# Row softmax steps on GpSimd and convolution evacuations on ScalarE, in a convolution and soft-MoE kernel

## The chip, the cores and the metric

One core of one Trainium2 chip runs the whole program. The metric is the device time of one execution in microseconds. TensorE (PE) multiplies matrices from SBUF into PSUM; VectorE (DVE) and ScalarE (ACT) copy PSUM to SBUF ("evacuate") and do elementwise work; GpSimd (POOL) works on SBUF; SyncE (SP) issues the DMAs.

## The reference

The input x is 8 batches of 3584 rows of 192 columns. A causal convolution over 7 rows, with one softmaxed set of weights for each of 8 heads (24 columns each), gives the rows of a soft mixture of experts with 32 slots (8 experts of 4 slots, hidden size 1024). The weights of the convolution are drawn eight times larger than in the function below.

```python
def _moe_ref(x, phi, w1, w2):
    logits = x @ phi                              # 28672 x 32
    d = softmax of logits over the 28672 rows     # dispatch
    slot_input = d.T @ x                          # 32 x 192
    slot_out[e] = relu(slot_input[e] @ w1[e]) @ w2[e]
    c = logits - logits.max(1, keepdims=True)     # row softmax over 32 slots
    c = np.exp(c)
    c /= c.sum(1, keepdims=True) + 1e-09
    return c @ slot_out                           # 28672 x 192
```

The row softmax c, in the last lines, is what the change touches first: one softmax over 32 numbers for each of the 28672 rows.

## The kernel before

All data are float32. The work of a batch is cut in two halves (n = 0 to 15 for 8 batches).

- **Convolution.** The even half of a batch uses `conv` (one 128x128 Toeplitz matrix a head, L522), the odd half `conv_units` (64x64 matrices, two heads at a time, L491, "units"). Results go through four PSUM banks `cv0` to `cv3` and are evacuated into the tiles `xc`. `conv` evacuates on ACT alone; `conv_units` on ACT or DVE. The copies are recorded at the helper's lines: L248 for ACT, L250 for DVE.
- **Turn and logits.** DVE transposes `xc` in 32x32 blocks into `xt` (L574, L580), PE computes the logits of the batch into the four banks of `lt` (L605).
- **Dispatch (`stage_b`).** DVE reads the logits, writes their negatives to `lall` and takes a running extremum (L629, L633); ACT takes the exponential into `dt` (L639); PE transposes it (L677); two copies of 128x512 bring it to SBUF as `dsb`, on ACT or DVE; PE accumulates the slots with it (L700) and DVE adds them to `ss` (L717).
- **Row softmax (`epath(j, u)`).** For each half batch u of batch j, 16 "softmax halves" in all, on 128x448 elements of `lall` in place: transpose (DVE, L763), minimum (L765), subtraction (L769), exponential (ACT, L773), sum, plus 1e-9 and reciprocal (DVE, L756 to L758), multiplication (L777), transpose back (L780). The small results lie in the tile `rmr`. This needs the logits of its batch and is needed only by the output of its batch.
- **Experts.** After the last batch the slots are normalized, multiplied with w1 and w2 (L871, L875, L916), scaled into `os` (L929) and spread over the partitions as `st` (L934).
- **Output.** For each batch PE multiplies `lall` with `st` (L957), alternating between the `cv` and the `lt` banks; ACT or DVE evacuates into `xc` buffers, which hold two batches; SP stores them (L982), 22 MB in all.

A planner fixes the order of instructions on every engine. Each step is added with a cost for each engine that may do it, the steps that it depends on, and a priority; where two engines may do a step, the planner takes the one that ends earlier by its costs. Steps with a priority of 1500 or more (the row softmax and the output) are fitted afterwards into the gaps that the others leave; POOL's memsets (x halo L460, L861) are planned in the same way. At run time every engine follows its order strictly, with semaphores between engines.

Of the kernel before, what the change touches and what calls it, by code (L numbers as in the profile page):

```python
# [12 lines left out]
ALU = mybir.AluOpType  # L13
# [4 lines left out]
class Plan:  # L18
# [16 lines left out]
    def add(self, fn, cost, reads=(), writes=(), prio=0.0, bias=0.15):  # L35
        i = len(self.steps)
        deps = set()
        for r in reads:
            if r in self.writer:
                deps.add(self.writer[r])  # L40
        for w in writes:
            if w in self.writer:
                deps.add(self.writer[w])
            deps.update(self.readers.get(w, ()))
        for r in reads:
            self.readers.setdefault(r, []).append(i)
        for w in writes:
            self.writer[w] = i
            self.readers[w] = []
        deps.discard(i)  # L50
        self.steps.append((fn, cost, deps, prio, bias, self.urgent))
        return i
# [125 lines left out]
def tile_conv_softmoe(ctx: ExitStack, tc: tile.TileContext, x, weight, phi, w1, w2, out):  # L178
    nc = tc.nc
# [34 lines left out]
    GT = TG * M  # L214
    NR = GT // RUN
    assert S == NG * GT and NR == P and HALO >= ZS
    NP = NT // 2
# [7 lines left out]
    def a_ps(n):  # L225
        return (n + 61) / 1200

    def a_sb(n):
        return (n + 112) / 1200

    def v_ps(n):
        return (n + 64) / 960

    def v_sb(n):
        return (n + 66) / 960
# [4 lines left out]
    def evac(n):  # L240
        return {"ACT": a_ps(n), "DVE": v_ps(n)}
# [4 lines left out]
    def copy(e, dst, src):  # L246
        if e == "ACT":
            nc.scalar.copy(dst, src)  # L248
        else:
            nc.vector.tensor_copy(dst, src)  # L250
# [17 lines left out]
    ltk, nvk = [f"lt{i}" for i in range(NB)], [f"ltn{i}" for i in range(NB)]  # L268
# [121 lines left out]
    for i in range(len(cuts) - 1):  # L390
# [3 lines left out]
            writes=[f"prod{i}"] + (alll + ["scr"] if i == 0 else []), prio=-3 + i,  # L394
        )
        add(band_sum(i), {"DVE": v_sb(HH * BW * KT)}, reads=[f"prod{i}"], writes=[f"band{i}"], prio=-3 + i)
        for u in range(2):
            for a, b in tk[u]:
                add(
                    band_put(i, a, b, u), {"ACT": a_sb(HH * U * 0.7), "DVE": v_sb(HH * U * 0.7)},  # L400
                    reads=[f"band{i}", ("tz", "tzu")[u], "scr"] + alll,
                    writes=[f"toe{'pu'[u]}{h}.{a}{b}" for h in range(cuts[i], cuts[i + 1])], prio=-3 + i + 6 * u,
# [65 lines left out]
    def rot(name, n):  # L468
        k = ring.get(name, 0)
        ring[name] = k + 1  # L470
        return f"{name}{k % n}"
# [7 lines left out]
    def conv_units(ch):  # L479
        pr = ch["n"] * 5  # L480
        CW = 2 * CG
        for h in range(0, H, 2):
            banks = [rot("cv", 4) for _ in range(2)]
            d0, d1 = h * CG, h * CG + CW
            pv = [ps[b][:, 0 : NP * CW].rearrange("p (q c) -> p q c", c=CW) for b in banks]

            def mm(e, h=h, pv=pv):
                for hh in range(h, h + 2):
                    for s, a in ((0, 0), (1, 1), (0, 1), (1, 0)):
                        rows = slice(UW * s, UW * (s + 1))  # L490
                        nc.tensor.matmul(  # L491
                            pv[s][UW * a : UW * (a + 1), :, (hh - h) * CG : (hh - h + 1) * CG], toeu[rows, hh, :],
                            ch["x"][rows, a:NT:2, hh * CG : (hh + 1) * CG], start=True, stop=True,
                        )

            add(
                mm, {"PE": 2 * NP * CG / 600 + 0.05},
                reads=[ch["xk"], ch["xk"] + "z"] + [f"toeu{hh}.{a}{b}" for hh in (h, h + 1) for a, b in tk[1]],
                writes=banks + [f"hd{ch['n']}.{hh}" for hh in (h, h + 1)], prio=pr,
            )  # L500
            for s in range(2):
                for w, lo, hi, o in (("a", d0, min(d1, P), s * (W2 - P)), ("b", max(d0, P), d1, 1 + s * D2)):
                    if lo >= hi:
                        continue

                    def ev(e, s=s, lo=lo, hi=hi, o=o, pv=pv, d0=d0):
                        copy(e, ch["xc"][:, :, o + lo : o + hi], pv[s][:, :, lo - d0 : hi - d0])

                    add(
                        ev, evac(NP * (hi - lo)), reads=[banks[s], "one"], writes=[f"{ch['xck']}.{h}{w}{s}"],  # L510
                        prio=pr,
                    )

# [72 lines left out]
    def stage_b(hs_):  # L586
# [3 lines left out]
        n, last = hs_[-1]["n"], hs_[-1]["n"] == 2 * B - 1  # L590
        tb, si, W = j * GT, len(stages), 4 * (h1 - h0) * U
        pr = n * 5 + 4.5
# [6 lines left out]
        for k in range(DB):  # L599

            def lg(e, k=k):
# [13 lines left out]
                reads=["phi"] + pace + [f"xt{hf}.{s}" for hf in range(h0, h1) for s in ((0, 1) if 32 * k < P else (2, 3))]  # L615
# [4 lines left out]
        lo = lall[:, tb : tb + GT].rearrange("p (r n b) -> p b n r", r=RUN, b=NB)[:, :, 4 * i0 : 4 * i1, :]  # L620
# [16 lines left out]
        for a0, a1 in parts:  # L637
# [6 lines left out]
                writes=[f"dt.{i}" for i in range(a0, a1, 4)], prio=pr,  # L644
# [28 lines left out]
        for a0, a1 in parts:  # L673

            def dtr(e, a0=a0, a1=a1):
# [5 lines left out]
                writes=nvk[a0 // 2 : a1 // 2], prio=late,  # L681
            )
        for b in range(i0 // 2, i1 // 2, 2):
            add(
                lambda e, b=b: copy(
                    e, dsb.rearrange("p (b k) n -> p b (k n)", k=2)[:, b : b + 2, :], nv[:, b : b + 2, :]
                ),
                evac(512), reads=nvk[b : b + 2], writes=[f"ds{b}"], prio=pr,
            )


        for a0, a1 in parts:

            def disp(e, a0=a0, a1=a1):
# [13 lines left out]
                reads=[f"ds{b}" for b in range(a0 // 2, a1 // 2, 2)] + ka, writes=[ltk[0], nvk[0]], prio=late,  # L708
# [36 lines left out]
    def epath(j, u, p0):  # L745


        n = 2 * j + u
        pr, GT = p0 + 20 * j, NR * RUN // 2
        lv = lall[:, n * GT : (n + 1) * GT]  # L750
        ev = lv.rearrange("p (a n) -> p a n", n=NS)
        rv, rk, lk = rmr[:, n % 4, 0 : GT // NS], f"r{n % 4}", f"l{j}.{u}"
        rb = rv.unsqueeze(2).broadcast_to((P, GT // NS, NS))

        def total(e):
            nc.vector.tensor_reduce(out=rv, in_=ev, axis=AX.X, op=ALU.add)  # L756
            nc.vector.tensor_scalar(out=rv, in0=rv, scalar1=1e-9, scalar2=None, op0=ALU.add)  # L757
            nc.vector.reciprocal(rv, rv)  # L758


        lp = lv.rearrange("p (t m b) -> p t b m", m=4, b=NB)
        ln = lv.rearrange("p (t b m) -> p t b m", m=4, b=NB)
        add(lambda e: nc.vector.transpose(ln, lp), {"DVE": v_sb(GT)}, reads=[lk], writes=[lk], prio=pr)  # L763
        add(
            lambda e: nc.vector.tensor_reduce(out=rv, in_=ev, axis=AX.X, op=ALU.min),  # L765
            {"DVE": v_sb(GT) + 0.1}, reads=[lk], writes=[rk], prio=pr,
        )
        add(
            lambda e: nc.vector.tensor_tensor(out=ev, in0=ev, in1=rb, op=ALU.subtract),  # L769
            {"DVE": v_sb(GT)}, reads=[lk, rk], writes=[lk], prio=pr,  # L770
        )
        add(
            lambda e: nc.scalar.activation(lv, lv, AF.Exp, scale=-1.0), {"ACT": a_sb(GT)}, reads=[lk], writes=[lk], prio=pr  # L773
        )
        add(total, {"DVE": v_sb(GT) + 0.4}, reads=[lk], writes=[rk], prio=pr)
        add(
            lambda e: nc.vector.tensor_tensor(out=ev, in0=ev, in1=rb, op=ALU.mult),  # L777
            {"DVE": v_sb(GT)}, reads=[lk, rk], writes=[lk], prio=pr,
        )
        add(lambda e: nc.vector.transpose(lv, lv), {"DVE": v_sb(GT)}, reads=[lk], writes=[lk], prio=pr)  # L780

# [6 lines left out]
    for n in range(2 * B + 1):  # L788
        if n == 2 * B - 1:
            plan.urgent = 0.4  # L790
        if n < 2 * B:
            (conv, conv_units)[n % 2](halves[n])
            if n + 3 < 2 * B:
                load_x(halves[n + 3])
        if n:
            ch = halves[n - 1]
            turn(ch)
            if ch["hf"]:
                stage_b(halves[n - 2 : n])
# [12 lines left out]
    for j in range(B):  # L812
        for u in range(2):
            epath(j, u, 1975 - 10 * u)
# [70 lines left out]
    op = ps["lt0"]  # L885
    for hf in range(HF):
# [24 lines left out]
        def l2(e, hf=hf):  # L911
# [14 lines left out]
            writes=["lt0"], prio=301.5,  # L926
# [17 lines left out]
    for j in range(B):  # L944
        tb = j * GT
        pr = 2000 + 20 * j + 5
        obs = [flat(xcr[(2 * j + a) % 4])[:, 0 : 2 * RUN * D].rearrange("p (k i d) -> p k i d", i=RUN, d=D) for a in range(2)]
        for i0 in range(0, RUN, 2):
            i1 = min(RUN, i0 + 2)
            banks = pok[npo % 2]  # L950
# [13 lines left out]
            for g in range(NG):  # L964
# [6 lines left out]
                w = [f"ob{oc}.{k}.{i0}"]  # L971
# [4 lines left out]
                if i1 in cutsw:  # L976

                    def store(e, g=g, k=k, lo=cutsw[i1], hi=i1, ob=obs[g // 2], j=j):
# [5 lines left out]
                    lo = cutsw[i1]  # L984
                    add(
                        store, dma((i1 - lo) * P * D * 4, (i1 - lo) * D * 4),
                        reads=[f"ob{oc}.{k}.{i}" for i in range(lo, i1, 2)], prio=pr + 0.1 * g,
# [31 lines left out]
```

## Time and profile before

| | |
|---|---|
| median of 3 runs | 265.89 us (262.21 to 265.9) |
| the profiled execution's own time | 263.53 us |
| its span | 261.7 us, 8162 instructions |
| busy time in the span | PE 213.6, DVE 196.8, ACT 110.0, POOL 7.2 us |
| mean granted TensorE clock | 0.854 |
| moved by DMA | 60.32 MB, 22.02 MB of it written |

A row of a timeline gives start, duration, engine, line, operation, tiles (out<-in) and count, and in brackets how long the engine stood idle before it and what released it. A table by stretches gives for each the busy time of each engine, with the number of instructions, then the granted clock, the share of the DMA engines' time and the GB/s.

The stages are: set-up to 18 us, a first batch filling the pipeline to 35, the loop over batches to about 155, the last dispatch and the experts to 192, the output to the end.

### The profile page before, as it was taken

What the parts mean: (1) busy time and instruction counts of PE and PEld (TensorE: products, weight loads), DVE (VectorE), ACT (ScalarE), POOL (GpSimd) and SP (SyncE); (2) the same over time, 40 slices, a digit from 0 to 9 for tenths busy, and PEclk for the clock granted to TensorE, in tenths of its full rate; (3) what the DMA queues carried; (4) which work ended last, traced back from release to release, by engine and by line L of the source; (5) the groups of instructions that cost most, each with busy time, mean ns of one, the idle gap of its engine ahead of it and who ended that gap; (6) DMA issues with size and microseconds to landing.
All of it is one profiled execution on the core that took longest, in us unless ns stands there. A gap on an engine that the chain in (4) does not pass through costs nothing. (4 is left out here: it accounts for less than half of the span.)

```text
span 261.7 us, 8162 instructions
## 1 busy us (share of the span) xinstructions
PE 213.6 (82%) x3474; PEld 129.5 (49%) x3474; DVE 196.8 (75%) x368; ACT 110.0 (42%) x277; POOL 7.2 (3%) x31
## 2 busy tenths in 40 slices
PE   6577999989989999999899787589777776786750
PEld 6334355355454464463463365455456655565630
DVE  3959299879889989989789579667878676974340
ACT  2675364363353454534445150422146443543340
POOL 5000000000000000000000002000000000000000
PEclk9689999999999999999999899689979755555555
DMA  5999969689489599499399879200028998797897
GB/s 165 248 262 237 274 161 238 206 185 281 181 194 285 206 217 336 138 222 295 82 231 247 269 241 347 87 3 3 3 90 285 360 395 334 286 372 297 337 350 271
DMA packets 52851, 60.32 MB, mean 230 GB/s; under 512 B 4304, under 2 KB 45136, under 8 KB 52816
## 3 DMA queue, kind: packets, MB, share of 16 engines
q1 hardware_dynamic: 52816, 59.81, 76.9%
q8 instruction: 27, 0.44, 0.7%
q14 instruction: 8, 0.07, 0.1%
HBM read 37.78 MB, written 22.02 MB: 228 GB/s over the span
## 5 line engine op out<-in xcount | busy, mean ns | idle before, releaser
L248 ACT COPY xc<-cv 128x384 f32<-128x384 f32 (+1 forms) x162 | 69.3, 456 | 85.9 <-PE cv L522 45.4
L522 PE MATMUL cv<-x,toep 128*128 128x384 f32 x128 | 57.3, 549 | 5.3 <-DMA x<-in_x_dram 3.5
L574 DVE STREAM_TRANSPOSE xt<-xc 128x1024 f32<-128x1024 f32 x32 | 37.9, 1221 | 9.5 <-PE lt L605 6.6
L957 PE MATMUL cv<-st,lall 32*128 32x192 f32 x256 | 33.0, 509 | 6.6 <-ACT xc L248 4.0
L605 PE MATMUL lt<-xt,phiq 32*32 32x224 f32 x1536 | 33.0, 360 | 5.0 <-issue 2.7
L522 PEld LDWEIGHTS cv<-x,toep 128*128 128x128 f32 x128 | 21.3, 197 | 27.7 <-issue 14.3
L957 PEld LDWEIGHTS cv<-st,lall 32*128 32x128 f32 x256 | 25.8, 286 | 11.6 <-ACT xc L248 7.0
L250 DVE COPY xc<-lt 128x192 f32<-128x192 f32 (+2 forms) x42 | 16.4, 422 | 18.9 <-ACT xc L248 16.0
L491 PE MATMUL cv<-x,toeu 64*64 64x192 f32 x512 | 29.9, 345 | 0.4 <-DVE xc L250 0.4
L250 DVE COPY xc<-cv 128x384 f32<-128x384 f32 (+2 forms) x54 | 25.0, 482 | 4.8 <-ACT xc L248 2.2
L957 PE MATMUL lt<-st,lall 32*128 32x192 f32 x192 | 21.5, 508 | 7.7 <-DVE xc L250 6.1
L605 PEld LDWEIGHTS lt<-xt,phiq 32*32 32x32 f32 x1536 | 12.9, 103 | 30.0 <-issue 22.6
L700 PE MATMUL lt<-xc,dsb 128*32 128x193 f32 x512 | 24.0, 342 | 3.5 <-DVE dsb L250 2.3
L491 PEld LDWEIGHTS cv<-x,toeu 64*64 64x64 f32 x512 | 19.9, 138 | 9.7 <-ACT xc L248 4.5
L700 PEld LDWEIGHTS lt<-xc,dsb 128*32 128x32 f32 x512 | 16.3, 114 | 12.6 <-DVE dsb L250 5.8
L957 PEld LDWEIGHTS lt<-st,lall 32*128 32x128 f32 x192 | 16.2, 294 | 11.7 <-ACT xc L248 5.7
L580 DVE STREAM_TRANSPOSE xt<-xc 128x512 f32<-128x512 f32 x32 | 20.6, 678 | 0.0
L248 ACT COPY xc<-lt 128x384 f32<-128x384 f32 (+2 forms) x30 | 10.8, 376 | 22.6 <-PE lt L957 15.6
L629 DVE TENSOR_SCALAR_CACHE_REDUCE lall<-lt 128x896 f32<-128x896 f32 x8 | 13.9, 1736 | 7.0 <-PE lt L605 7.0
L763 DVE STREAM_TRANSPOSE lall<-lall 128x448 f32<-128x448 f32 x16 | 15.2, 961 | 0.0
L639 ACT ACTIVATE dt<-lt,small 128x896 f32<-128x896 f32 (+1 forms) x9 | 8.2, 925 | 12.1 <-DVE lall L629 9.9
L677 PE MATMUL lt<-ident,dt 128*128 128x128 f32 x64 | 9.6, 298 | 3.9 <-ACT dt L639 3.9
(95 smaller groups left out, 166.2 us busy)
## 6 DMA issues: line engine op xcount, KB each, us to landing
x<-in_x_dram SPq DMA_DIRECT2D x64, 192.0 KB, 4.7
x<-in_x_dram SPq DMA_DIRECT2D x24, 384.0 KB, 6.5
out_dram<-xc SPq DMA_DIRECT2D x24, 384.0 KB, 4.1
out_dram<-xc SPq DMA_DIRECT2D x24, 288.0 KB, 3.8
x<-in_moe_w_dram SPq DMA_DIRECT2D x6, 768.0 KB, 6.7
out_dram<-xc SPq DMA_DIRECT2D x24, 192.0 KB, 2.0
w1a<-in_moe_w_dram SPq DMA_DIRECT2D x8, 512.0 KB, 8.0
x<-in_x_dram SPq DMA_DIRECT2D x8, 288.0 KB, 5.2
```

The source lines that it names most:

```text
L248: nc.scalar.copy(dst, src)
L250: nc.vector.tensor_copy(dst, src)
L491: nc.tensor.matmul(pv[s][UW * a : UW * (a + 1), :, (hh - h) * CG : (hh - h + 1) * CG], toeu[rows, hh, :], ch["x"][rows, a:NT:2, hh * CG : ...
L522: nc.tensor.matmul(pv, toep[:, h, :], ch["x"][:, :, d0:d1], start=True, stop=True)
L574: lambda e, s=s, o=o: nc.vector.transpose(xa[:, s, :, :, 0:P], xg[:, :, :, o : o + P]),
L580: lambda e, s=s, o=o: nc.vector.transpose(xa[:, s, :, :, P:D], xg[:, :, :, o : o + D2]),
L605: nc.tensor.matmul(lt[g * NS : (g + 1) * NS, b, 0:W], phiq[rows, k, :], xt[rows, h0:h1, 4 * g : 4 * g + 4, 32 * k : 32 * k + U], start=(k ...
L629: nc.vector.tensor_scalar(out=lo, in0=li, scalar1=-1.0, scalar2=None, op0=ALU.mult, op1=ALU.min, accum_out=cm)
L677: nc.tensor.transpose(nv[:, i // 2, i % 2 * P : (i % 2 + 1) * P], dt_[:, i, :], ident)
L700: nc.tensor.matmul(sp[g * NS : (g + 1) * NS, o : o + D1], dsb[:, i, g * NS : (g + 1) * NS], xc[:, 2 * g + k, s * D1 : (s + 1) * D1], start ...
L763: add(lambda e: nc.vector.transpose(ln, lp), {"DVE": v_sb(GT)}, reads=[lk], writes=[lk], prio=pr)
L957: nc.tensor.matmul(ps[banks[g]][:, (i - i0) * 256 : (i - i0) * 256 + D], lall[rows, tb + i * NR : tb + (i + 1) * NR], st[rows, :], start=T ...
```

## The change

Three edits. The evacuations of `conv_units` may be done on ACT only. The copies into `dsb` may be done on ACT only, except for the last batch's. The subtraction (L769) and the multiplication (L777) of the row softmax go from DVE to POOL, with a planned cost of 1.0 us each; before, the planned cost on DVE was (448 + 66)/960, 0.54 us. The planner makes a new order with these costs.

```diff
 # conv_units
                     add(
-                        ev, evac(NP * (hi - lo)), reads=[banks[s], "one"], writes=[f"{ch['xck']}.{h}{w}{s}"],
+                        ev, {"ACT": a_ps(NP * (hi - lo))}, reads=[banks[s], "one"], writes=[f"{ch['xck']}.{h}{w}{s}"],
                         prio=pr,
                     )
 # stage_b
-                evac(512), reads=nvk[b : b + 2], writes=[f"ds{b}"], prio=pr,
+                evac(512) if last else {"ACT": a_ps(512)}, reads=nvk[b : b + 2], writes=[f"ds{b}"], prio=pr,
 # epath
         add(
-            lambda e: nc.vector.tensor_tensor(out=ev, in0=ev, in1=rb, op=ALU.subtract),
-            {"DVE": v_sb(GT)}, reads=[lk, rk], writes=[lk], prio=pr,
+            lambda e: nc.gpsimd.tensor_tensor(out=ev, in0=ev, in1=rb, op=ALU.subtract),
+            {"POOL": 1.0}, reads=[lk, rk], writes=[lk], prio=pr,
         )
...
         add(
-            lambda e: nc.vector.tensor_tensor(out=ev, in0=ev, in1=rb, op=ALU.mult),
-            {"DVE": v_sb(GT)}, reads=[lk, rk], writes=[lk], prio=pr,
+            lambda e: nc.gpsimd.tensor_tensor(out=ev, in0=ev, in1=rb, op=ALU.mult),
+            {"POOL": 1.0}, reads=[lk, rk], writes=[lk], prio=pr,
         )
```

## The prediction

> **What bounds the kernel now.** I read the page's span first, then the stages: a table of busy times by stretch (columns: stretch, its length, then PE, PEld, DVE, ACT, POOL busy with instruction counts, granted clock, DMA share, GB/s).
>
> ```profile
> span 261.7 us, 8162 instructions
> ...
> 35.00:155.00 120.00, 112.02 (x2136) 58.66 (x2132) 103.04 (x164) 55.02 (x125) 1.24 (x5) 0.99 0.85 225
> 155.00:192.00 37.00, 28.38 (x582) 18.61 (x586) 30.03 (x66) 7.85 (x21) 1.81 (x1) 0.91 0.26 87
> 192.00:207.00 15.00, 12.32 (x150) 10.39 (x150) 10.83 (x24) 8.17 (x21) 0.00 (x0) 0.77 0.71 258
> 207.00:216.00 9.00, 6.54 (x56) 4.95 (x56) 7.14 (x13) 4.38 (x12) 0.00 (x0) 0.64 1.02 394
> 216.00:237.00 21.00, 15.92 (x130) 12.13 (x130) 16.19 (x37) 9.25 (x24) 0.00 (x0) 0.50 0.84 324
> 237.00:252.00 15.00, 11.34 (x111) 9.88 (x112) 6.96 (x16) 6.33 (x16) 0.00 (x0) 0.50 0.89 342
> ```
>
> The loop over the batches (35 to 155 us) is PE's: 112.0 of 120 us at full clock, so at most 8 us can be won there, whatever happens to DVE, which is 86% busy, or ACT, at 46%. From 192 us on the output is written. At 207 to 216 us the DMA engines are full (394 GB/s); after that they have holes (0.84, 0.89), PE runs at half clock, and the two stretches differ in one thing: up to 237 us DVE still does softmax work between the evacuations. How much, the instructions that touch the small statistics tile rmr show (six of the eight DVE steps of one softmax half, so 96 for 16 halves):
>
> ```profile
> 35.00:155.00 120.00, 19.32 (x40) 0.99 0.85 225
> 155.00:192.00 37.00, 14.71 (x33) 0.91 0.26 87
> 192.00:262.00 70.00, 11.36 (x24) 0.58 0.84 316
> ```
>
> 24 of 96, so four halves' worth of sixteen, are done while output is being written. What they cost there is read from PE, in order of time: each of these rows is the start of a batch of output, with the wait in front of it (the first three at higher clock, before DMA limits; the batch between 202.27 and 220.38 has no such clean row).
>
> ```profile
> 191.86 1.20 PE L957 MATMUL cv<-st,lall 32*128 32x192 f32 x16 [0.41 <-ACT st L248]
> ...
> 197.03 1.41 PE L957 MATMUL cv<-st,lall 32*128 32x192 f32 x16
> ...
> 202.27 1.82 PE L957 MATMUL cv<-st,lall 32*128 32x192 f32 x15
> ...
> 220.38 1.66 PE L957 MATMUL lt<-st,lall 32*128 32x192 f32 x16 [1.43 <-ACT xc L248]
> ...
> 229.30 1.66 PE L957 MATMUL lt<-st,lall 32*128 32x192 f32 x16 [1.41 <-DVE xc L250]
> ...
> 238.15 1.66 PE L957 MATMUL lt<-st,lall 32*128 32x192 f32 x16 [1.45 <-DVE xc L250]
> ...
> 246.13 1.66 PE L957 MATMUL lt<-st,lall 32*128 32x192 f32 x16 [1.42 <-DVE xc L250]
> ```
>
> A batch takes 8.92 and 8.85 us while softmax halves are in the way, 7.98 us when they are done, at the same clock of 0.50. 22.02 MB in 8 batches at 394 GB/s is 6.99 us of DMA each, so PE and its evacuations set the pace after 216 us.
>
> **The change, part by part.** First POOL's price. The trace of before has no two-input POOL instruction; the rows nearest to it, and the DVE rows it replaces (columns: line, engine, operation, shapes, count | busy us, mean ns | idle before):
>
> ```profile
> L769 DVE TENSOR_TENSOR lall<-lall,rmr 128x448 f32<-128x448 f32 x16 | 9.9, 616 | 0.2
> ...
> L777 DVE TENSOR_TENSOR lall<-lall,rmr 128x448 f32<-128x448 f32 x16 | 10.0, 624 | 0.4
> ...
> L861 POOL MEMSET xc<- 128x2048 f32 x1 | 1.8, 1810 | 44.8 <-PE lt L700 44.8
> ...
> L321 POOL MEMSET toep<- 128x1024 f32 x1 | 0.9, 945 | 0.0
> ...
> masks.py:199 POOL TENSOR_SCALAR_AFFINE_SELECT ident<-ident 128x128 f32<-128x128 f32 x1 | 0.3, 292 | 0.1
> ```
>
> The memsets give 0.845 ns an element ((1810-945)/1024) and 80 ns fixed, so 448 elements cost at least 0.46 us. The select, which reads and writes, takes (292-80)/128 = 1.66 ns an element; two reads at twice that give 3.3 ns, 1.56 us, the upper end. I take the select plus one more stream at the memsets' rate, 2.5 ns: 1.2 us. It hides nowhere by itself, since it stands in a chain (minimum, subtract, exponential, sum, scale, transpose), but the halves have until 192 us and other work lies on every engine meanwhile; 32 x 1.2 = 38 us on an engine that is now 3% busy.
> The Trainium skill, GPSIMD Engine Reference, section 3.1, measures 4497 ns for such an instruction of 2048 elements, as an estimate 984 ns for 448; its section 4.1 says not to put elementwise work there, being about twice as slow as VectorE. No run here shows it yet; by its figure the sum stays the same, since both prices lie below the point at which the slower rival starts.
>
> DVE's budget in the loop. Moved away are its 33 PSUM copies there and 40/96 of L769 and L777 (19.9 us), 8.3 us. These copies, and the transposes that stay:
>
> ```profile
> 35.00:155.00 120.00, 14.63 (x33) 0.99 0.85 225
> ...
> L763 DVE STREAM_TRANSPOSE lall<-lall 128x448 f32<-128x448 f32 x16 | 15.2, 961 | 0.0
> ...
> L780 DVE STREAM_TRANSPOSE lall<-lall 128x448 f32<-128x448 f32 x16 | 10.3, 643 | 0.4
> ```
>
> 14.6 + 8.3 = 22.9 us come free, beside 17 us that are idle now. A half costs DVE 45.38/16 = 2.84 us of rmr steps (19.32 + 14.71 + 11.36 = 45.4 us) and 1.60 of transposes, 4.44 us; without the two moved steps 3.20. The four late halves need 12.8 us and fit. That is the whole of what the change can do: **it moves four halves out of the output stage.**
>
> (1) Loop. PE's waits in 35 to 155 us that end on the engines concerned, and the end of such a chain in one period:
>
> ```profile
> PE lt L677 <- ACT dt L639: 3.3, 6, 0.6
> PE lt L605 <- issue: 2.7, 2, 1.8
> PE lt L700 <- DVE dsb L250: 1.2, 5, 0.2
> ```
> ```profile
> 39.12 1.07 ACT L248 COPY dsb<-lt 128x512 f32<-128x512 f32 x2 [0.27 <-PE lt L677]
> ...
> 76.07 0.59 ACT L248 COPY dsb<-lt 128x512 f32<-128x512 f32 x1
> ...
> 76.69 0.69 DVE L250 COPY dsb<-lt 128x512 f32<-128x512 f32 x1 [0.82 <-ACT dsb L248]
> ...
> 77.44 0.37 PE L700 MATMUL lt<-xc,dsb 128*32 128x193 f32 x4 [0.25 <-DVE dsb L250]
> ```
>
> DVE's half of dsb starts only when ACT's is done, so two copies back to back on ACT (1.07 us at 39.12) replace 1.31 (76.07 to 77.38). ACT then carries in this phase the maximum's exponential, eight unit evacuations and both dsb copies. With dsb ahead of the last unit evacuations it ends near 76.9 and PE's 0.25 us goes; with all of them ahead it ends up to 1 us later, of which PE hides half behind convolution. I take -1.0 us for the loop (most of the 1.2), bounds -2 and +3.5 (0.5 in seven periods). The 3.3 us wait for the exponential stays: its reduction waits for PE's logits, not for DVE; so do the 2.7 us of PE's own issue. With dsb gone, that exponential is the next thing late.
>
> (2) End of the loop. Here no convolution covers PE:
>
> ```profile
> 155.35 2.83 PE L700 MATMUL lt<-xc,dsb 128*32 128x193 f32 x64 [1.09 <-DVE dsb L250]
> ...
> 159.05 3.70 PE L605 MATMUL lt<-xt,phiq 32*32 32x224 f32 x192 [0.87 <-DVE ss L717]
> ```
>
> An earlier dsb, and a DVE that no longer evacuates just ahead of its transposes, take about half of 1.96 us: -1.0 (0 to -2).
>
> (3) Before the output, the expert product's last matmul ends at 189.5 us, but:
>
> ```profile
> 189.19 0.33 PE L916 MATMUL lt<-xc,xc 128*32 128x192 f32 x1
> ...
> 189.87 0.61 DVE L765 TENSOR_REDUCE rmr<-lall 128x14 f32<-128x448 f32 x1
> ...
> 190.39 0.41 DVE L929 TENSOR_SCALAR os<-lt,small 128x192 f32<-128x192 f32 x1
> ```
>
> The scaling waits 0.9 us behind a softmax reduction. With the halves done earlier -0.6 (0 to -0.9).
>
> (4) Output. The fifth and sixth batch (from 220.38 and 229.30) go from 8.9 to 7.98 us, -1.8. The two batches ahead of them took 18.1 us from 202.27 to 220.38; at 7.98 each that is -2.1. Sum -3.9, I take -3.8. Bounds: 0, if stores rather than evacuations hold them (207 to 216 us is full), and -9, below.
>
> Queues. POOL is in order: the memset of x's halo (L460, seven times) now stands behind subtractions that wait for DVE, and SP's x load and all later loads behind that memset. In the loop PE never waits for x, so a delay of about 1 us costs nothing; without that slack it would be its own length, seven times. ACT's exponential of a half (L773) now waits for POOL, with evacuations queued behind it and PE behind those; four cv banks cover four heads in the 128-row phase, two pairs in the unit phase, so there it shows first. DVE's sum and last transpose wait for ACT and POOL, with the x transposes behind them.
>
> Sum: -1.0 - 1.0 - 0.6 - 3.8 = -6.4 us on the profiled execution's 263.53 us (span 261.7 and 1.8 around it): 257.1. That execution is 2.4 us below the median shown, 265.89, and within the 262.21 to 265.9 of the runs; I add 1.4, 258.5. About 2%, 5.3 us, is what a measurement can tell from no change.
>
> **Rivals.** *Nothing from the output stage.* The planner could still place late halves there, or the stores' order keeps its holes: only (1) to (3), or one of them, remain: 263.53 - 2.6 + 1.4 = 262.3. For it: 8 to 9 us of DVE's loop time falls in pieces that a 0.96 us transpose must fit between; against it: DVE is nearly free from 164 to 190 us as well.
> *PE's clock stays up.* At the first batches PE took 5.17 us a batch (191.86 to 197.03). If shorter stalls keep the clock there, DMA sets 6.99 us a batch: against 7.98 another 5 us, so -9 in (4): 253.5. For it: the clock is 0.77 where batches follow closely; against it: 0.50 in 237 to 252 us, where no softmax is left.
> The Trainium skill, TensorE: Matmul & The Clock Gate, part 1, has the clock drop after idle windows of some 3.4 us; in the rows above it is down although PE's waits are 1.4 us, so the trace doesn't bear that out, and I leave this rival small.
> *Slower: POOL's operation is long, and DVE stands behind it.* A period, from the reduction that opens each batch:
>
> ```profile
> L629 DVE TENSOR_SCALAR_CACHE_REDUCE lall<-lt x8: 1655/1747/1753, 35.1 to 162.8; 128x896 f32<-128x896 f32 x8
> ```
>
> (162.8 - 35.1)/7 = 18.2 us, 6.6 in the loop. DVE needs (103.0 - 14.6 - 19.3 - 6.7 halves x 1.60 of transposes)/6.6 = 8.85 us of it beside two halves at 3.2, so 2.95 are idle. Four POOL results a period are waited for in DVE's order, laid out for about 1.2 us each. Beyond 1.2 + 2.95/4 = 1.94 us DVE becomes the bound; at 2.4 us (twice my value) the loop grows by (4 x 1.2 - 2.95) x 6.6 = 12 us: 263.5 + 12 - 1.6 + 1.4 = 275. Against it: the upper end of 1.56 from the rows. For it: an operand broadcast over 32 elements is in none of them.
> The Trainium skill, GPSIMD Engine Reference, section 1, has POOL share its SBUF interface with VectorE, with contention for DVE instructions of two SBUF inputs; the big ones of these are the two that move away, so by it little is left to collide, and no run here shows it.
> That the change doesn't do what it says is excluded for its engines, which are fixed in the code; the order is the planner's, and is the first rival.
>
> **How the numbers follow.** Forecast 0.53 (its own range 255 to 261), first rival 0.28, clock 0.09, slower 0.10. The range must leave out no more than 0.2: it drops the slower case and part of the clock's, and runs from 253.5 to 265.5 (the first rival with the loop's loss). Faster by over 2% (below 260.6): 0.45 of the forecast's and the clock's 0.09, 0.54. Slower by over 2%: 0.09. The rest, 0.37, is within.
>
> **What would show it.** POOL's instructions at 1.0 to 1.5 us; no rmr step after 192 us; batches of output 8.0 us apart at clock 0.50; PE waiting for dsb under 0.25 us a period; the scaling right behind the expert product. Wrong I am if DVE or ACT waits long for POOL in the loop, if PE waits for unit evacuations, or if the output's DMA share doesn't rise above 0.9.

## The result, and the profile after

The changed kernel takes 254.49 us (median of 4 runs, 251.84 to 255.67), the kernel before 264.9 (4 runs, 262.21 to 265.9). The ratio is 0.959, with a 95% interval of 0.947 to 0.971; the run of 255.67 us counts as a slow one and isn't in it. The forecast was 258.5 us, with a range of 253.5 to 265.5. The profiled execution took 254.35 us.

First the page's span and the table by stretch of the kernel after, the same columns as before (length, then PE, PEld, DVE, ACT, POOL busy, granted clock, DMA share, GB/s):

```profile
span 252.6 us, 8180 instructions
...
35.00:155.00 120.00, 112.30 (x2192) 60.18 (x2188) 96.87 (x152) 69.28 (x164) 24.16 (x30) 1.00 0.88 228
155.00:192.00 37.00, 29.01 (x578) 19.18 (x566) 19.30 (x46) 8.58 (x24) 8.32 (x8) 0.91 0.25 86
192.00:207.00 15.00, 10.74 (x135) 8.52 (x138) 9.28 (x21) 8.01 (x21) 0.00 (x0) 0.78 0.90 335
207.00:216.00 9.00, 6.55 (x70) 5.57 (x66) 3.49 (x8) 3.28 (x8) 0.00 (x0) 0.50 1.02 392
216.00:237.00 21.00, 15.03 (x179) 12.42 (x176) 10.46 (x24) 9.91 (x25) 0.00 (x0) 0.74 1.01 388
```

PE's share of the loop is unchanged (112.0 and 112.3 of 120 us). The holes of the DMA engines are gone: 0.84 has become 1.01 in 216 to 237 us, and the granted clock there is 0.74 instead of 0.50. The instructions on rmr (now DVE's and POOL's) show what left the output stage:

```profile
35.00:155.00 120.00, 19.15 (x49) 23.07 (x25) 1.00 0.88 228
155.00:192.00 37.00, 5.64 (x15) 6.51 (x7) 0.91 0.25 86
192.00:262.00 70.00, 0.00 (x0) 0.00 (x0) 0.69 0.83 312
```

None is left in the output stage, where there were 24. The batches of output, each with the wait in front of it, in PE's order of time:

```profile
189.01 0.93 PE L957 MATMUL cv<-st,lall 32*128 32x192 f32 x16 [0.41 <-ACT st L248]
...
214.38 1.66 PE L957 MATMUL lt<-st,lall 32*128 32x192 f32 x16 [1.47 <-DVE xc L250]
...
221.27 1.66 PE L957 MATMUL lt<-st,lall 32*128 32x192 f32 x16 [1.42 <-DVE xc L250]
...
228.19 1.66 PE L957 MATMUL lt<-st,lall 32*128 32x192 f32 x16 [1.46 <-DVE xc L250]
...
235.18 1.66 PE L957 MATMUL lt<-st,lall 32*128 32x192 f32 x16 [1.47 <-DVE xc L250]
```

They are 6.9 to 7.0 us apart, close to the 6.99 us that a batch's stores take at 394 GB/s. But it is not the stores that hold PE there. The evacuations, on which PE waits 1.4 us as before, wait for a store only twice after 200 us (total, times, longest):

```profile
ACT xc L248 <- DMA out_dram<-xc: 2.1, 1, 2.1
```
```profile
DVE xc L250 <- DMA out_dram<-xc: 0.4, 1, 0.4
```

What differs from the 7.98 us of before is the granted clock, 0.74 to 0.75 in the batches from 214.38 to 235.18 us instead of 0.50. The stores run behind PE: the last evacuation ends at 243.1 us, and SP is still issuing stores until 249.65 (start, duration, count):

```profile
240.08 9.57 SPq L982 DMA_DIRECT2D out_dram<-xc  x17
```

The second place where time went is at 146 us. PE's order of time before, then after; "issue" in the last bracket says that PE waited for nothing that the profile shows:

```profile
145.59 0.64 PE L605 MATMUL lt<-xt,phiq 32*32 32x224 f32 x26
148.03 0.96 PE L605 MATMUL lt<-xt,phiq 32*32 32x224 f32 x6 [1.80 <-issue]
```
```profile
145.75 0.64 PE L605 MATMUL lt<-xt,phiq 32*32 32x224 f32 x26
146.66 0.57 PE L605 MATMUL lt<-xt,phiq 32*32 32x224 f32 x6 [0.26 <-issue]
```

And the reductions that open the sixth and the seventh batch on DVE, before, then after:

```profile
128.02 1.75 DVE L629 TENSOR_SCALAR_CACHE_REDUCE lall<-lt 128x896 f32<-128x896 f32 x1 [1.85 <-PE lt L605]
...
149.05 1.74 DVE L629 TENSOR_SCALAR_CACHE_REDUCE lall<-lt 128x896 f32<-128x896 f32 x1 [3.03 <-PE lt L605]
```
```profile
128.11 1.75 DVE L629 TENSOR_SCALAR_CACHE_REDUCE lall<-lt 128x896 f32<-128x896 f32 x1 [1.52 <-PE lt L605]
...
147.28 1.75 DVE L629 TENSOR_SCALAR_CACHE_REDUCE lall<-lt 128x896 f32<-128x896 f32 x1 [1.10 <-PE lt L605]
```

With these marks the 9.1 us between the two spans fall so:

| stretch | before | after | difference |
|---|---|---|---|
| start to the first batch's reduction | 35.07 | 34.99 | -0.1 |
| five periods, first to sixth reduction | 92.95 | 93.12 | +0.2 |
| sixth to seventh | 21.03 | 19.17 | -1.9 |
| seventh to eighth | 13.79 | 13.55 | -0.2 |
| eighth reduction to the first output matmul | 29.02 | 28.18 | -0.8 |
| output: first four batches | 28.52 | 25.37 | -3.2 |
| fifth and sixth batch | 17.77 | 13.81 | -4.0 |
| seventh batch to the end | 23.55 | 24.41 | +0.9 |

### The profile page after: what moved, and what is told of

The parts are those of the page before. It is cut to its first block, busy times and chain, and to the rows that moved or that the text cites. A ratio compares the mean times of both kernels' runs of the same rounds, so it can differ in the third digit from the quotient of the medians.

```text
span 252.6 us, 8180 instructions
## 1 busy us (share of the span) xinstructions
PE 204.7 (81%) x3474; PEld 124.4 (49%) x3474; DVE 163.1 (65%) x302; ACT 121.1 (48%) x311; POOL 36.6 (15%) x63
## 5 line engine op out<-in xcount | busy, mean ns | idle before, releaser
L248 ACT COPY xc<-cv 128x384 f32<-128x384 f32 (+2 forms) x195 | 78.1, 457 | 65.8 <-PE cv L522 46.7
L522 PE MATMUL cv<-x,toep 128*128 128x384 f32 x128 | 55.9, 545 | 5.4 <-DMA phiq<-in_moe_phi_dram 3.6
L574 DVE STREAM_TRANSPOSE xt<-xc 128x1024 f32<-128x1024 f32 x32 | 37.7, 1216 | 22.9 <-PE lt L605 13.4
L605 PE MATMUL lt<-xt,phiq 32*32 32x224 f32 x1536 | 32.9, 359 | 4.0 <-DVE ss L717 1.6
L250 DVE COPY xc<-lt 128x192 f32<-128x192 f32 (+2 forms) x47 | 18.5, 428 | 25.9 <-ACT xc L248 19.5
L957 PE MATMUL cv<-st,lall 32*128 32x192 f32 x256 | 27.0, 447 | 4.2 <-ACT xc L248 3.8
L605 PEld LDWEIGHTS lt<-xt,phiq 32*32 32x32 f32 x1536 | 13.0, 103 | 29.2 <-issue 20.9
L957 PE MATMUL lt<-st,lall 32*128 32x192 f32 x192 | 19.7, 470 | 9.5 <-DVE xc L250 9.5
L957 PEld LDWEIGHTS cv<-st,lall 32*128 32x128 f32 x256 | 21.5, 255 | 8.5 <-ACT xc L248 7.0
L777 POOL TENSOR_TENSOR lall<-lall,rmr 128x448 f32<-128x448 f32 x16 | 15.0, 939 | 64.0 <-DVE rmr L758 44.4
L957 PEld LDWEIGHTS lt<-st,lall 32*128 32x128 f32 x192 | 14.5, 265 | 12.4 <-DVE xc L250 4.4
L248 ACT COPY xc<-lt 128x384 f32<-128x384 f32 (+2 forms) x25 | 9.0, 369 | 22.5 <-PE lt L957 10.9
L250 DVE COPY xc<-cv 128x384 f32<-128x384 f32 x21 | 11.3, 553 | 6.6 <-PE cv L957 5.7
L769 POOL TENSOR_TENSOR lall<-lall,rmr 128x448 f32<-128x448 f32 x16 | 15.0, 939 | 2.4 <-DVE rmr L765 2.4
L763 DVE STREAM_TRANSPOSE lall<-lall 128x448 f32<-128x448 f32 x16 | 15.1, 947 | 0.0
```

The source lines that it names most:

```text
L522: nc.tensor.matmul(pv, toep[:, h, :], ch["x"][:, :, d0:d1], start=True, stop=True)
L574: lambda e, s=s, o=o: nc.vector.transpose(xa[:, s, :, :, 0:P], xg[:, :, :, o : o + P]),
L605: nc.tensor.matmul(lt[g * NS : (g + 1) * NS, b, 0:W], phiq[rows, k, :], xt[rows, h0:h1, 4 * g : 4 * g + 4, 32 * k : 32 * k + U], start=(k ...
L769: lambda e: nc.gpsimd.tensor_tensor(out=ev, in0=ev, in1=rb, op=ALU.subtract),
L777: lambda e: nc.gpsimd.tensor_tensor(out=ev, in0=ev, in1=rb, op=ALU.mult),
L957: nc.tensor.matmul(ps[banks[g]][:, (i - i0) * 256 : (i - i0) * 256 + D], lall[rows, tb + i * NR : tb + (i + 1) * NR], st[rows, :], start=T ...
```

## The experiments

My theory after the result: the halves that left the output stage give the larger part, and PE's shorter stall at 146 us the second. The rivals: POOL itself is what helps, or DVE's relief from evacuations, or the new order of loads on SP. Each run stands against runs of the kernel before that were made along with it: 259.53 to 266.55 us (7 runs, median 264.65) for e1, e2, e4 and e9; 261.55 to 265.8 (7, 263.77) for e5, e6, e7b and e8; 260.98 to 265.68 (13, 262.99) for e7a and e10 to e12.

**Each part alone.** `e1_pool_only` undoes the two edits of the evacuations; `e2_act_only` has only those.

```diff
 # e1: after, with
-   ev, {"ACT": a_ps(NP * (hi - lo))}, reads=[banks[s], "one"], ...
+   ev, evac(NP * (hi - lo)), reads=[banks[s], "one"], ...
-   evac(512) if last else {"ACT": a_ps(512)}, reads=nvk[b : b + 2], ...
+   evac(512), reads=nvk[b : b + 2], ...
 # e2: after, with both gpsimd.tensor_tensor of epath as
+   nc.vector.tensor_tensor(...), {"DVE": v_sb(GT)}
```

> Only the row softmax's subtraction and multiplication go to POOL; unit evacuations and dsb copies may use ACT or DVE as before. Theory (late halves): the gain is that no softmax half is left for the output stage, so that the stores keep the DMA engines full there; either part of the change frees enough of DVE for that. Here all but one transpose is ordered ahead of the output: 254 to 257 us, DMA share about 1.0 from 201 us to the end. Rival (chain): the gain is the shorter dsb and evacuation chain on ACT: then 263 to 265. Rival (clock): the output stage was faster since PE's clock happened to be higher there: 254 to 265, with no tie to the number of late halves.

> Only the unit evacuations and dsb copies are tied to ACT; the softmax stays on DVE. Late halves: DVE is freed of 14.6 us in the loop, which holds three of the four late halves; one sum, one multiplication and one transpose are ordered after the output's start: 255 to 258 us. Rival (POOL's part carries the gain): 263 to 265. Rival (chain): 254 to 256.

e1 took 259.78 us (257.38 to 260.18), e2 254.18 (252.76 to 255.09). So the evacuations alone bring the whole gain. POOL alone brings about half by the medians, but the kernel before also ran in 259.53 us, so the size of that share is not clear of the scatter. Neither has a softmax half in the output stage (in e1 the last steps end ahead of the output's start at 194.68; in e2 only one multiplication and one transpose come after 187.86), so either part makes the room: the output takes 63.7 us in the trace of e1 and 64.5 in that of e2, against 69.8 before. What parts them comes earlier: PE's stalls on issue at L605 come to 3.7 us in e1 and 0.2 in e2. The stall at this place and the start of the output in e1, then in e2:

```profile
149.56 0.96 PE L605 MATMUL lt<-xt,phiq 32*32 32x224 f32 x6 [2.32 <-issue]
...
194.68 0.93 PE L957 MATMUL cv<-st,lall 32*128 32x192 f32 x16 [0.41 <-ACT st L248]
```
```profile
144.58 0.57 PE L605 MATMUL lt<-xt,phiq 32*32 32x224 f32 x6 [0.16 <-issue]
...
187.86 0.93 PE L957 MATMUL cv<-st,lall 32*128 32x192 f32 x16 [0.41 <-ACT st L248]
```

**The evacuations of conv_units free again.** `e9_units_free` is the kernel after with one edit undone, so POOL's two steps and the copies of the exponentials on ACT stay.

```diff
-   ev, {"ACT": a_ps(NP * (hi - lo))}, reads=[banks[s], "one"], ...
+   ev, evac(NP * (hi - lo)), reads=[banks[s], "one"], ...
```

> The changed kernel with the unit evacuations free again (ACT or DVE); softmax on POOL and dsb on ACT stay. PE's order then has a convolution head ahead of the dispatch product again, as before, and no late half. Late halves with the loop bound by PE: the 0.41 us wait for dsb in each of six periods of the changed kernel goes, so 1.5 to 2.5 us less than the changed kernel: 252 to 253 us. Rival (evacuations on ACT alone are themselves a gain): 256 to 259.

257.36 us (255.75 to 258.36). Here the copies of the exponentials on ACT do what my first step said: PE's wait for them in 35 to 160 us is

```profile
PE lt L700 <- ACT dsb L248: 0.4, 1, 0.4
```

and the four periods from the first to the fifth reduction take 72.3 us against 73.3 in e1, which differs from it in these copies alone. In the kernel after they take 73.55, and PE waits for dsb 0.4 us in every period: with the unit evacuations on ACT too, the planner puts the dispatch ahead of the next head's convolution, and the convolution no longer covers the wait. The profiled executions of e9 and after differ by 4.0 us: e9 loses 2.0 in the period that ends with the seventh batch's reduction, where it has a stall of 2.61 us, 1.9 ahead of the first reduction, 1.3 in the output and 0.6 in between, and its five periods win 1.8 back.

**Is it the order of the loads?** In the kernels without the pinned evacuations (before, e1, e9) SP issues most of w1b behind the last x loads; in after and e2 more of it goes ahead of them. `e5_before_loads_early` and `e6_units_free_loads_early` are before and e9 with the loads of w1 planned as shorter, to bring that order about.

```diff
 def load_w(key, dst, src, nbytes, prio):
-    add(..., dma(nbytes, F * 4), writes=[key], prio=prio)
+    add(..., {"DMA": 0.85 * nbytes / 360e3}, writes=[key], prio=prio)
```

> The kernel before with one number changed: the planned cost of the w1 loads times 0.85. PE, DVE, ACT and POOL keep their order to the instruction; SP alone issues the weight loads in the order of the kernel after, ahead of the last x loads. Theory A (the pin of the unit evacuations works through this load order: in the kernels before, e1 and e9 PE stands 1.8 to 2.6 us on its own issue at 147 to 149 us, behind bulk loads, and not in after and e2): the stall in L605 falls from 1.8 to below 0.5 us, the output starts 1.5 to 3 us earlier than 191.9, the four late halves stay in the output, and the time is 1.5 to 3 us below that of before. Theory B (the stall comes from the order on PE or from DVE's copies): stall 1.8 us as before, time within 0.5 us of before.

> The kernel after with unit evacuations on ACT or DVE (that of e9, which took 257.4 with a 2.6 us stall of PE's issue at 149 us) and the planned cost of the w1 loads times 0.85; the other engines keep the order of e9. Theory A (load order makes the stall): stall below 0.5 us, 254.0 to 255.5, so equal to after; with e9's shorter period (18.1 against 18.45 us) perhaps 253. Theory B (order on PE makes it): 257.4 again.

e5 took 267.97 us (ratio 1.016, 1.006 to 1.025), so it lost where a gain was expected; e6 took 257.64, no better than e9. The order moved only part of the way: of the eight w1b loads three go ahead of the last x loads in e5 and four in e6, against one in before and e9 and five in after. So far as it moved it brought nothing, and the load order as the lever is not borne out. The trace of e5 shows what happened instead, in PE's order of time:

```profile
149.92 0.57 PE L605 MATMUL lt<-xt,phiq 32*32 32x224 f32 x6 [1.20 <-issue]
...
164.73 1.82 PE L605 MATMUL lt<-xt,phiq 32*32 32x224 f32 x80 [1.68 <-issue]
```

The stall shrank (1.80 to 1.20) and a new one of 1.68 us came in the last dispatch, where before has none; e6 has the same pair (1.3 and 2.2). Of the 4.2 us that e5 lost, the stalls, with a third of 1.74 us near 128 us where before has 0.87, explain about 2; its first reduction is 1.4 us later in the profiled execution, and the rest stays open. A list of DMA queues by stretch suggests what PE waits for. One packet of PE's instruction queue falls in 145 to 146 us before, and in 144 to 145 after; the rows give queue, packets, MB and share of the 16 engines:

```profile
q8 instruction: 1, 0.02, 6.9%
```
```profile
q8 instruction: 1, 0.02, 6.6%
```

In before, after, e1, e2, e5, e6, e8, e9, e10 and e12 PE breaks off at the same place, 26 matmuls into a group of 32, which fits the end of a block of instructions; it goes on 2.5 to 3.5 us after the start of the microsecond in which the packet moved. Before and after reach that place within 0.2 us of each other (146.23 and 146.39); the packet of before comes more than a microsecond later (about 145.4 and 144.0 us). In e5 and e6 the second stall stands in the same way behind a packet at 162 and 158 us, inside a stretch of w2 loads that fills the engines (1.06). The Trainium skill, Runtime: NRT & Kernel Launch, section "Instruction fetch mechanics", has each engine refilled in 16 KiB blocks of 256 instructions through a DMA queue of its own, and calls the crossing of a block mostly hidden. The traces agree with the block (27 packets, 0.44 MB on this queue) but not always with the hiding: 0.2 to 2.6 us here.

**Less load.** `e10_before_w2_cut`, `e11_after_w2_cut` and `e12_units_free_w2_cut` cut the eight w2 loads to a twenty-fourth, in before, after and e9.

```diff
-   dst.rearrange("p (q c) -> p q c", c=FQB * D), w2[e].rearrange("(q p b) d -> p q (b d)", p=P, b=FQB)
+   dst.rearrange("p (q c) -> p q c", c=FQB * D)[:, 0, 0:64],
+   w2[e].rearrange("(q p b) d -> p q (b d)", p=P, b=FQB)[:, 0, 0:64],
```

> The kernel before with each of the eight loads of w2 (L739, 786 KB each) cut to its first 64 columns of the first row block (33 KB); place and order stay, the experts' result is not the reference's. In the traces so far PE's 16 KB packets of instructions go through the same DMA engines: in before one of them moves between 145 and 146 us, while w2 loads fill the engines (1.08), and PE stands from 146.2 to 148.0; in after it moves a microsecond earlier against PE's need and PE stands 0.26. Theory A (PE's instructions queue behind the bulk loads): the 1.8 us stall goes to under 0.3, the output starts 2 to 3 us earlier than 191.9, the time falls by 2 to 3 us against before, the output stage stays at 68 us and more with its late halves. Theory B (the stall is PE's own, from its program): 1.8 us as before, time within 1 us of before.

> The kernel after with the same cut of the w2 loads (experts' result not the reference's). Theory A (after already escapes the queue): PE's stalls on issue there are 0.3 us, so the time stays within 0.8 us of after (254.5) and the gap between before and after in the start of the output (2.85 us) closes to under 1 us against e10. Theory B (after gains by its order on the engines): the start of the output in e10 and here still differs by 2 us and more.

> e9 (the kernel after, unit evacuations on ACT or DVE; 257.4) with the same cut of the w2 loads. Theory A (what the pinned unit evacuations gave over e9 is the missing stall alone, and e9's loop is shorter by 0.35 us a period): stall 2.6 to under 0.3 us, 253.5 to 254.8, at or below e11. Theory B (the pinned evacuations help by themselves): 256 and more, and above e11 by 2 us.

The same place of PE in e10, then in e12:

```profile
147.69 0.57 PE L605 MATMUL lt<-xt,phiq 32*32 32x224 f32 x6 [0.97 <-issue]
```
```profile
145.15 0.57 PE L605 MATMUL lt<-xt,phiq 32*32 32x224 f32 x6 [1.05 <-issue]
```

The stalls fell (1.80 to 0.97 and 2.61 to 1.05; e11 has no break there at all), but not to the 0.3 us that I expected: the last x and w1b loads still fill the engines to 145 us in e10. In all three pairs less load goes with a shorter stall, in one execution of each; that the load makes the stall is likely, but not shown. In before the engines are full (0.98 to 1.08) up to 145 us, but the microsecond in which the packet moves has a share of 0.75, not the 1.08 that I had read there, and in the stall itself it is 0.29 and 0.65. In time, e10 took 262.34 us (ratio 0.997, 0.993 to 1.001), not 2 to 3 us less: its output starts at 190.8, 1.1 us earlier, and still takes 70.1 us. e11 took 253.69 (0.963, 0.956 to 0.970) and e12 254.14 (0.966, 0.960 to 0.971), so e9's distance to after, 2.9 us, closes to 0.5 with the load. The starts of the output in e10 and e11 differ by 1.3 us, between the two theories. Most of the 8.7 us that part e10 from e11 is thus in the output stage.

**The late halves themselves.** `e8_no_late_halves` is before without the row softmax of the last two batches.

```diff
-    for j in range(B):
+    for j in range(B - 2):
         for u in range(2):
             epath(j, u, 1975 - 10 * u)
```

> The kernel before with the row softmax of the last two batches left out (four halves of sixteen; in the kernel before these four are the ones that stand in the output stage). Theory A (late halves make the output of before long, 69.8 us against about 64 in after, e1 and e2): output 63.5 to 65 us and DMA share near 1.0, time 4 to 6 us below before, PE's 1.8 us stall unchanged. Theory B (my prediction's own sum: evacuations and half clock set 7.98 us a batch): 3 to 4 us below before, batches 8 us apart at a clock of 0.50. Theory C (the output stage of before is long for another reason, the order of its stores): under 1 us.

256.8 us, ratio 0.972 (0.960 to 0.983): 7.0 us (4.6 to 10.4 by the interval), somewhat above theory A, and the stall stays (2.1). Its instructions on rmr after 192 us, its table for 216 to 237, and its last four batches:

```profile
192.00:262.00 70.00, 0.00 (x0) 0.69 0.84 316
```
```profile
216.00:237.00 21.00, 15.03 (x152) 12.18 (x151) 10.33 (x24) 9.38 (x23) 0.00 (x0) 0.58 1.02 391
```
```profile
213.59 1.66 PE L957 MATMUL lt<-st,lall 32*128 32x192 f32 x16 [1.50 <-DVE xc L250]
...
221.53 1.66 PE L957 MATMUL lt<-st,lall 32*128 32x192 f32 x16 [1.42 <-DVE xc L250]
...
229.50 1.66 PE L957 MATMUL lt<-st,lall 32*128 32x192 f32 x16 [1.47 <-DVE xc L250]
...
236.49 1.66 PE L957 MATMUL lt<-st,lall 32*128 32x192 f32 x16 [1.47 <-DVE xc L250]
```

The output takes 63.9 us instead of 69.8. Its batches take 7.94, 7.97 and 6.99 us, both of the values that I had weighed, in one execution. The DMA engines stay full in either (a share of 1.02 in each of these batches). So a few batches of 8 us cost nothing as long as the stores run behind PE; in before the batches of 8.9 us left holes, and the next, of 8.0 us, did too (0.90).

The other way round, `e4_four_late` puts the halves of the last two batches of the kernel after back into the output, all on DVE.

```diff
+    add(lambda e: nc.vector.transpose(ln, lp), {"DVE": v_sb(GT)}, reads=[lk] + (["st"] if late else []), ...)
...
-    for j in range(B):
+    for j in range(B - 2):
         for u in range(2):
             epath(j, u, 1975 - 10 * u)
...  # before the output; subtraction and multiplication on DVE when late
+    for j in range(B - 2, B):
+        for u in range(2):
+            epath(j, u, 1975 - 10 * u, late=True)
```

> The changed kernel, but the four softmax halves of the last two batches may only begin when st is there, and run wholly on DVE (as the four late halves of before did). Late halves: 17.8 us of DVE come back between the evacuations: 259 to 263 us, DMA share with holes again (0.8 to 0.9 after 216 us). Rival (clock): nothing but scatter, 252 to 256. Rival (the loop carries the gain): 254 to 255.

Three of its four runs took 253.74 to 256.68 us (median 254.75), so about what after takes; the fourth took 259.62 at a lower mean clock (0.854 against 0.88 to 0.90), and it is the only one with a trace. Late halves alone are thus not enough to lose 7 us, and what the output stage of the three looked like is not on record. A low clock alone is not enough either. In e9 PE is granted 0.50 from 216 us on, its batches are 8 us apart, and the DMA engines stay full (a table by stretch of e9, then one batch of after):

```profile
216.73:224.65 7.92, 5.99 (x56) 5.00 (x57) 3.49 (x8) 3.28 (x8) 0.00 (x0) 0.50 0.99 377
224.65:232.62 7.97, 5.99 (x56) 5.00 (x57) 3.49 (x8) 3.28 (x8) 0.00 (x0) 0.50 1.02 392
232.62:240.66 8.04, 5.99 (x57) 5.01 (x57) 3.49 (x8) 3.28 (x8) 0.00 (x0) 0.50 0.99 378
```
```profile
221.27:228.19 6.92, 4.94 (x56) 4.07 (x57) 3.48 (x8) 3.28 (x8) 0.00 (x0) 0.75 1.02 394
```

The output of e9 takes 64.9 us, that of after 63.6. At like clocks it is the late halves that part the traces: before, at 0.50 in 216 to 237 us, has a DMA share of 0.84, and e10, which has the halves too, has holes at the 0.58 at which e8 had 1.02:

```profile
216.00:237.00 21.00, 14.96 (x130) 11.31 (x130) 16.16 (x37) 9.33 (x24) 0.00 (x0) 0.58 0.83 318
```

So the traces put the holes down to the late halves. Why e4's faster runs escape them, by a higher clock or by the place of the steps among the evacuations, stays open, as does why PE is granted 0.50 in one stretch and more in another.

**POOL's price.** `e7a_pool_half_again` and `e7b_pool_long` put one and three more subtractions of a broadcast zero on POOL ahead of each half's own.

```diff
-   lambda e: nc.gpsimd.tensor_tensor(out=ev, in0=ev, in1=rb, op=ALU.subtract),
+   lambda e: ([nc.gpsimd.tensor_tensor(out=ev, in0=ev, in1=<zeros>, op=ALU.subtract) for _ in range(1)],  # e7b: 3
+              nc.gpsimd.tensor_tensor(out=ev, in0=ev, in1=rb, op=ALU.subtract)),
```

> The kernel after with three more subtractions on POOL (of a broadcast zero) ahead of each half's own, planned at nothing, so that every engine keeps its order and a half's POOL work takes 4.7 us instead of 1.88. Theory of the prediction's slower rival (DVE waits in order behind POOL; DVE has about 2.95 us of slack a period, reached at 7.8 us of POOL a period): a period takes 9.4 us of POOL, so the loop grows by (9.4 - 7.8) x 6.6 = 10.8 us, to about 265, with DVE's waits on POOL of 3 us and more a period. Other theory (the planner put enough other DVE work between POOL's result and its reader): under 3 us of loss, POOL busy near 127 us.

> The kernel after with one more subtraction (of a broadcast zero) on POOL ahead of each half's own: 2.82 us of POOL a half instead of 1.88, order unchanged. The slower rival's point was 1.94 us an operation, 3.88 us a half; three more subtractions (4.70 us a half) cost 14 us, with ACT, not DVE, standing behind POOL for 39.7 us in the loop. Theory A (a point as the rival put it, near 3.9 us): no loss, within 1.5 us of 254.5. Theory B (ACT stands behind every microsecond, about 14.2/2.82 = 5 us of loss for 1 us a half): 259 to 260, with ACT's wait for POOL in the loop growing from 1.5 us to over 10.

e7a took 254.85 us (ratio 0.966, 0.961 to 0.972, against 0.959 of after): no loss. e7b took 268.65 (1.019, 1.009 to 1.029), 14 us more than after. ACT's wait for POOL in the loop in e7a, then in e7b, and PE's largest wait in e7b (35 to 155 us; total, times, longest):

```profile
ACT lall L773 <- POOL lall L769: 13.6, 12, 1.4
```
```profile
ACT lall L773 <- POOL lall L769: 39.7, 12, 4.1
...
PE lt L677 <- ACT dt L639: 9.6, 6, 2.3
```

So there is a point, between 2.8 and 4.7 us of POOL a half; ACT's 13.6 us of waiting are free, 39.7 are not. It is ACT that stands behind POOL, and PE behind ACT's exponential.

## Why the prediction was right, and where it wasn't

The measured 254.49 us lies in the range of 253.5 to 265.5, but half a microsecond below the 255 to 261 that I gave the forecast by itself: the terms add up to -6.4 us where the spans differ by 9.1. Some of the signs that I named did not come: the batches are not 8.0 us apart, and PE waits for dsb 0.41 us a period, not under 0.25.

**What bounds the kernel; four halves leave the output.** Right: none is left there, and every trace without these halves (after, e1, e2, e6, e7a, e7b, e8, e9, e11, e12) has an output of 63.5 to 64.9 us, where before, e5 and e10, with four, have 69.8 to 70.7. e8 prices them at 7.0 us of the 10.4, but with their work left out altogether; put back into the changed kernel (e4) they cost next to nothing in three runs of four. So that price is the price in the kernel before and not one of the halves as such. POOL was not needed for it: of the 22.9 us of DVE time that I added up, the 14.6 of the copies are enough (e2).

**(4) Output, -3.8 us: mis-sized, measured -6.25.** The failed step is the 7.98 us a batch: I took the distance between PE's batches, which the kernel before showed at a clock of 0.50, for what sets the end of the output. It doesn't. In e9 PE keeps that pace and the output takes 64.9 us; in after the batches are 6.9 us apart and it takes 63.6. As long as the stores run behind PE, the full DMA engines set the end. The sum should have gone by the holes of before: at 394 GB/s they are worth, as an estimate from the table in the prediction, 21 x (1 - 324/394) + 15 x (1 - 342/394) = 5.7 us in 216 to 252 us. By batches, the fifth and sixth gave 4.0 us instead of my 1.8 and the first four 3.2 instead of 2.1; 0.9 came back at the end, where stores drain after the last matmul. The rival to which I gave 0.09 had the right bound, the DMA engines, but tied it to a PE clock that stays up, which e9 doesn't need, and its -9 was too much.

**(1) Loop, -1.0 us: the size nearly held (-1.9 + 0.2), by luck; the cause didn't.** The copies on ACT do give about 1.0 us (e9 against e1), but not together with the unit evacuations: PE's dsb wait in 35 to 160 us, the last one with it, stayed as long, 2.3 us before and 2.4 after (waits of PE of after):

```profile
PE lt L700 <- ACT dsb L248: 2.4, 6, 0.4
PE lt L605 <- DVE ss L717: 1.6, 1, 1.6
PE lt L605 <- issue: 0.8, 2, 0.5
```

The 1.9 us of the period before the seventh batch are PE's stall there (1.80 to 0.26) and the six matmuls behind it (0.96 to 0.57). I had written off PE's waits on issue as staying (2.7 us in the loop); they fell to 0.8. Nothing in the edits touches them, so I put that down to where the packet and the loads came to lie, which is argued and not shown.

**(2) End of the loop, -1.0 us: too large, measured -0.2.** The last of the dsb waits there fell from 1.09 to 0.41 us (after):

```profile
152.69 2.83 PE L700 MATMUL lt<-xc,dsb 128*32 128x193 f32 x64 [0.41 <-ACT dsb L248]
157.09 3.69 PE L605 MATMUL lt<-xt,phiq 32*32 32x224 f32 x192 [1.57 <-DVE ss L717]
```

but the wait for ss grew from 0.87 to 1.57. **(3) The scaling, -0.6 us: right**, -0.8 with the stretch around it. PE's wait for os, before and after:

```profile
PE cv L934 <- DVE os L929: 1.3, 1, 1.3
```
```profile
PE cv L934 <- DVE os L929: 0.6, 1, 0.6
```

**POOL's 1.2 us: too high, within its bounds.** The rows of after:

```profile
L777 POOL TENSOR_TENSOR lall<-lall,rmr 128x448 f32<-128x448 f32 x16 | 15.0, 939 | 64.0 <-DVE rmr L758 44.4
...
L769 POOL TENSOR_TENSOR lall<-lall,rmr 128x448 f32<-128x448 f32 x16 | 15.0, 939 | 2.4 <-DVE rmr L765 2.4
```

Of the Trainium skill's GPSIMD Engine Reference, section 3.1 holds here (an estimate of 984 ns by its figure, 939 measured); the factor of about two of its section 4.1 is 1.5 here (939 against 616 and 624 ns). The contention of its section 1 is hardly put to the test: the large two-input instructions left DVE, and its transposes L763 take 947 ns after 961. **The slower rival** put its point at 3.9 us a half and its price at 10.8 us for e7b; the runs are in keeping with the point (between 2.8 and 4.7 us) and give 14. It named DVE as the engine that stands behind POOL, and there it was wrong: that is ACT, whose exponential I had listed under the queues alone.

## What to carry to other kernels

Before pricing work that leaves an output stage, divide the bytes by the rate of a stretch in which the DMA engines are full: once the holes are gone, that sets the end, and a PE whose batches are slower costs nothing while stores are queued. A part that frees an engine can be replaced by another that frees it as well (here either of two was enough to clear the output stage), so test each alone before calling one the cause. A stall on issue moved in almost every kernel here in which the order moved; take it as a term of some 2 us of either sign in a kernel like this one, and look for it in the trace before explaining a difference of that size.

## What the runs showed of the hardware that I had not expected

Instructions come in packets of 16 KB through the same DMA engines as the data (27 on one queue in before, which I take for PE's by its number of instructions), and PE stands on issue until some 3 us after such a packet moves: 0.2 to 2.6 us at one and the same place of the program, up to 2.2 us at another. That a full DMA queue delays the packet fits the rows, but e10 has a stall of 0.97 us too, with the engines all but idle from 146 us on. After the stall of 1.8 us in the kernel before, the next stretch ran at half clock; after the 0.97 us in e10 the clock stayed at 1.00:

```profile
149.00:151.00 2.00, 2.00 (x28) 1.56 (x32) 1.91 (x4) 0.46 (x2) 0.00 (x0) 0.50 1.07 395
```
